# A four-layer attention and Fourier kernel: the Fourier transform in eight equal chunks, the last three of the first layer by blocks of rows

## The chip, the cores and the metric

The kernel runs on one core of one Trainium2 chip. A core has four engines that compute (TensorE does matrix multiplies; VectorE, ScalarE and GpSimd do the rest; in the profile they are PE, DVE, ACT and POOL), a fifth, SyncE, that here issues every DMA (SP), and 16 DMA engines. The metric is device time in microseconds: 1803.18 us is the median of three runs before the change (1801.92 to 1805.65).

## The reference

The input x has 2048 rows of 512 numbers. Four sublayers follow each other: attention A, Fourier mixing B, attention A again with the same weights, Fourier mixing B again. In this text an A with the B behind it is a layer, so there are layer one and layer two.

```
x = x + A(layernorm(x));  x = x + B(layernorm(x));  x = x + A(layernorm(x));  x = x + B(layernorm(x))

A(x): q, k, v = x@wq, x@wk, x@wv          # 32 heads of 16, rows cut into N = 4 segments of 512
  for s in range(4):                       # M, z: a memory carried from segment to segment
    p     = softmax(q_s k_s^T * scale + mask);   a_dot = p v_s
    a_mem = (phi(q_s) M) / (phi(q_s) z + 1e-6)
    o_s   = g * a_mem + (1 - g) * a_dot
    M, z += phi(k_s)^T v_s, sum phi(k_s)
  return concat(o) @ wo

B(x): a = x @ hid_re^T;  b = x @ hid_im^T        # [2048, 512] each
      y = seq_re @ a - seq_im @ b                # [2048, 2048] by [2048, 512], twice
```

What matters here: attention goes segment by segment of 512 rows, but each row of B's result needs all 2048 rows of its input. So layer two's attention can start on a row only when all rows of layer one have been through B.

## The kernel before

**Work.** A row tile is 128 rows, so there are 16 row tiles; a segment q (0 to 7, four to a layer) has four of them and is worked on in four groups of eight heads. Group i = 4q + g (0 to 31) goes through these steps, each a generator in the code: `s_p` projects q and k from the normalised, transposed rows (`xt`, tiles named g0 and g1) and `s_v` projects v; `t_split` stores q and k in two float16 halves to DRAM and loads them stacked (`qst`, `kst`, two sets); `s_x` multiplies all scores once and `t_max` takes the row maxima on VectorE; a transpose and two small DMAs put the maxima into `qst`; `s_st` multiplies the scores again, transposed, `t_sel` takes the exponential on ScalarE and masks on GpSimd (tiles of kind `pt`); `s_av` multiplies them with v; `s_m` divides (`t_merge`, through four DMAs) and adds the memory's share. A segment's four results `ot` then go through `s_o`: for each row tile WO, the product with wo, then `t_res`, which adds the residual and starts y with it (or adds to it), and `t_ln`, the layer norm, which ends in a transposing DMA into `xb`.

**Fourier mixing.** `s_ab` multiplies a row tile's `xb` with the hidden-side matrices into two float16 pairs `ab` (24 matmuls of 512 columns, called AB here). `s_f` does the sequence side. Its contraction runs over the 16 input row tiles, cut into chunks by `CHUNKS`; for each chunk and each output row tile t (a unit) a PSUM tile takes 12 matmuls for each pair of input row tiles, and `t_y` adds the PSUM tile into y[t]: VectorE's `scalar_tensor_tensor` (ScalarE writes it where it is the first). Before the change the chunks are six of 2 row tiles and one of 4. A unit of the 4-wide chunk is 24 matmuls. After the last chunk `t_y` stores y[t] to DRAM (x1 in layer one, the output in layer two). The sequence matrices come as pieces of 256 KB: `s_r` loads one (`craw`), `s_c` scales and splits it into float16 halves (`cc`), and stores those for layer two.

**Order.** No engine chooses its order on the chip. A planner (class `Plan` and the loop from line 1086) runs when the program is built: it lets the generator go next whose inputs, buffers and engine are free soonest by its own costs, and each engine then executes its instructions in that order, waiting at each for its inputs. Buffers come from 50 slots of 128 x 512 words (`work`, tiles named w) and 8 PSUM banks (tiles named b); `setup` gives each kind a least and a greatest number, and `slots_free` keeps back what other kinds have not yet got of their least. All instructions are recorded on one line, that of a helper, L241 (`Eng.call`), so tile names tell them apart.

**Where layer two starts.** `s_ln` of segment 4, the first of layer two, waits for each of its four rows' ("y", 0, t), loads them again from x1 and normalises them; then `s_p` can start group 16. Layer two's `s_o` waits once, at segment 4, until all 16 y tiles of layer one are stored:

```
            if layer and s == 0:
                yield gate(("y", layer - 1, NT - 1))
                ywritten.clear()
```

Of the kernel before, what the change touches and what calls it, by code (L numbers as in the profile page):

```python
# [19 lines left out]
NT = S // 128  # L20
# [6 lines left out]
CHUNKS = [2] * 6 + [4]  # L27
# [8 lines left out]
BATCH = 4  # L36
NR = 2


class Plan:  # L40
# [4 lines left out]
    def __init__(self):  # L45
# [8 lines left out]
        self.by = {}  # L54
        self.dma = None
# [22 lines left out]

    def slots_free(self, kinds):
        extra, taken, r = {}, {}, 0.0  # L80
        for k in kinds:
# [166 lines left out]
def body(ctx: ExitStack, tc: tile.TileContext, x, wq, wk, wv, wo, beta, wd, cs, out):  # L248
# [14 lines left out]
        ab=(4, 12)))  # L263
# [58 lines left out]
    def gate(*keys):  # L322
        return lambda: all(k in done for k in keys)
# [531 lines left out]
    def s_av():  # L855
        for i in range(NGRP):
# [16 lines left out]
            done.add(("E", i))  # L873

# [21 lines left out]
    def t_res(p, xi, gt, xb, key, last):  # L896
        yield need("V", p, xi)
        first = gt not in ywritten
        xo = y[:, gt, :] if first else xi
        V.scalar_tensor_tensor(xo, p, f_o, xi, op0=OP.mult, op1=OP.add)  # L900
        ywritten.add(gt)
# [37 lines left out]
    units = [(j, t) for j in range(len(chunks)) for t in range(NT)]  # L939
    nunit = len(CHUNKS) * NT  # L940
    npiece = NT * PAIRS
    cct = [tc.dram_tile([128, 2, 512], F16, name=f"cc{u}") for u in range(npiece)]
# [7 lines left out]
    def s_r():  # L950
        yield gate("WO")
        for j, t in units[:nunit]:
            for gt in chunks[j][1][::2]:
                yield need("Y", tag="craw")
                raw = sb("craw")
                Y.dma_start(raw, cs[gt // 2, t])
                raws.append(raw)
        u = npiece
        for k in range(npiece):
# [8 lines left out]
    def s_c():  # L968
        k = u = 0
        while u < nunit:  # L970
            n = width(units[u][0])
# [34 lines left out]
            u += m  # L1006

# [25 lines left out]
    def t_y(p, layer, t, f, last):  # L1033
        if t not in ywritten:
            ywritten.add(t)
# [6 lines left out]
        if last:  # L1042
            yield need("Y", y)
            Y.dma_start(fins[layer][t], y[:, t, :])
            done.add(("y", layer, t))

    def s_f():
        u = 0
        for j, (layer, r) in enumerate(chunks):
            pl.area["ab"]["kinds"]["ab"] = 2 * max(len(c[1]) for c in chunks[j:j + 2]), 12  # L1050
            keys = [(layer, gt, e) for gt in r for e in range(2)]
            yield gate(*[("ab", *k) for k in keys])
            ab = [abs_.pop(k) for k in keys]
            n = len(r) // 2
            for t in range(NT):
# [14 lines left out]
                f = (j % len(CHUNKS)) * NT + t  # L1070
# [101 lines left out]
```

## Time and profile before

| | |
|---|---|
| median of three runs | 1803.18 us (1801.92 to 1805.65) |
| the profiled execution | span 1799.7 us from first to last instruction; no other time of this execution is given |
| PE busy | 1689.9 us, 94% of the span, 11045 matmuls |
| DVE, ACT, POOL busy | 1090.5, 897.4, 726.2 us (61, 50, 40%) |
| DMA | 242.43 MB, mean 135 GB/s |
| mean granted TensorE clock | 0.971 |

The page divides the span into 40 slices of 45 us. Rows of stages give busy time of each engine (in brackets the number of instructions), then the granted TensorE clock, the busy share of the 16 DMA engines and GB/s. Rows of groups give engine, operation, output and inputs, shapes, count, then busy time and mean duration in ns, then the idle time ahead of them with what ended it. Rows of the order in time give start, duration, engine, operation, tiles, count, and in brackets the idle time ahead with its releaser. A busy PE is not PE at its peak: a matmul that runs at half the clock is busy for twice as long.

In the text, F(j, t) is the unit of chunk j and output row tile t, P, V, X, ST and AV are a group's projection, v, first scores, second scores and product with v, and "P16" is P of group 16.

### The profile page before, as it was taken

The page shows a single profiled execution, that of the slowest core. Times are in us where ns is not written, and L with a number is a line of the kernel's source. Part 1 is how long each engine was busy: PE and PEld are TensorE (multiplying, and loading weights), DVE is VectorE, ACT ScalarE, POOL GpSimd, SP SyncE. Part 2 cuts the span into 40 slices and gives each one's busy share as a digit, 9 for nine tenths or more (in the row PEclk, how much of TensorE's full clock was granted, in tenths as well). Part 3 has the DMA queues.
Part 4 walks back from the last instruction along what each step waited for, and adds up shares of the span by engine and source line. Part 5 has one row for each costly group of instructions (what it writes and reads, how often), then busy time and mean ns, then how long its engine had stood idle before and what let it go on. Part 6 is the DMA issues. An engine that isn't in the chain of part 4 may idle for free.

```text
span 1799.7 us, 32605 instructions
## 1 busy us (share of the span) xinstructions
PE 1689.9 (94%) x11045; PEld 741.6 (41%) x11045; DVE 1090.5 (61%) x3405; ACT 897.4 (50%) x1563; POOL 726.2 (40%) x1157
## 2 busy tenths in 40 slices
PE   3877899999999999999999879999999999999999
PEld 1432344443444444444444333444444444444444
DVE  7797865768587677464566655554637566534211
ACT  2547668656656666635437555465344444441000
POOL 3225554546554554543425443442534333332000
PEclk8888899999999999999999888999999999999999
DMA  7345645665565453544875442752526533232233
GB/s 193 98 123 137 187 113 151 175 158 148 134 167 165 131 139 118 151 133 157 263 184 172 125 127 49 158 142 78 141 88 141 147 108 103 80 103 65 94 123 117
DMA packets 240984, 242.43 MB, mean 135 GB/s; under 512 B 129777, under 2 KB 152305, under 8 KB 240817
## 3 DMA queue, kind: packets, MB, share of 16 engines
q1 hardware_dynamic: 240816, 240.35, 48.5%
q8 instruction: 87, 1.43, 0.3%
q14 instruction: 81, 0.66, 0.1%
HBM read 152.96 MB, written 63.70 MB: 120 GB/s over the span
## 4 chain that ended last, share of the span: by engine, by line
PE 63%; DMA 11%; DVE 10%; ACT 5%; issue 5%; POOL 4%; SPq 3%; ACTq 0%; POOLq 0%; DVEq 0%
PE b L241 63%; ACT w L241 5%; DMA w<-w 3%; DVE junk L241 3%; SPq L241 3%; POOL w L241 3%; DVE w L241 2%; DMA dc<-den 2%; DMA w<-rec 1%; DMA den<-w 1%; DVE cam L241 1%; DMA rec<-dc 1%; DMA w<-in_cs_dram 1%; DVE mx L241 1%; DVE y L241 1%
## 5 line engine op out<-in xcount | busy, mean ns | idle before, releaser
L241 PEld LDWEIGHTS <-w 128*128 128x128 f16 x4992 | 467.0, 99 | 625.7 <-issue 120.6
L241 PE MATMUL b<-w,w 128*128 128x512 f16 x3072 | 708.9, 380 | 2.9 <-DVE w L241 1.4
L241 POOL TENSOR_TENSOR w<-w,w 128x512 f16<-128x512 f32 (+1 forms) x317 | 381.3, 1208 | 388.6 <-ACT w L241 236.7
L241 ACT ACTIVATE w<-b,fac 128x512 f32<-128x512 f32 (+1 forms) x728 | 420.4, 657 | 185.3 <-PE b L241 180.0
L241 DVE CUSTOM_DVE_ANT_0 junk<-b,cmask 128x128 bf16<-128x128 f32 (+3 forms) x1024 | 438.3, 484 | 76.1 <-PE b L241 75.2
L241 POOL TENSOR_SCALAR_AFFINE_SELECT w<-w 128x128 f32<-128x128 f32 (+2 forms) x704 | 245.4, 360 | 342.5 <-ACT w L241 330.4
L241 DVE SCALAR_TENSOR_TENSOR y<-b,fyu,y 128x512 f32<-128x512 f32 x200 | 149.2, 746 | 212.7 <-PE b L241 211.9
L241 ACT ACTIVATE w<-b 128x512 f32<-128x512 f32 (+1 forms) x240 | 137.0, 597 | 215.2 <-PE b L241 208.9
L241 ACT ACTIVATE w<-w,csc 128x512 f16<-128x512 f32 (+1 forms) x256 | 181.5, 722 | 62.3 <-DVE csc L241 56.8
L241 PE MATMUL b<-g,w 128*128 128x512 f16 x768 | 187.1, 388 | 9.9 <-issue 5.3
L241 PE MATMUL b<-w,vt 128*32 128x512 f32 (+3 forms) x2048 | 183.3, 459 | 2.9 <-POOL w L241 2.1
L241 PE MATMUL b<-wd,w 128*128 128x512 f16 x768 | 177.7, 379 | 0.6 <-ACT y L241 0.5
L241 ACT ACTIVATE w<-w 128x512 f16<-128x512 f32 (+1 forms) x144 | 90.2, 632 | 166.2 <-DVE w L241 119.6
L241 DVE SCALAR_TENSOR_TENSOR w<-b,w 128x512 f16<-128x512 f32 x128 | 87.7, 687 | 128.1 <-ACT w L241 125.7
L241 PE MATMUL b<-kst,qst 62*128 62x128 f16 (+3 forms) x1024 | 130.2, 312 | 17.3 <-DVE mx L241 9.2
L241 PE MATMUL b<-qst,kst 64*128 64x512 f16 (+3 forms) x1024 | 120.8, 306 | 13.3 <-DVE mx L241 5.6
L241 PE MATMUL b<-w,g 128*128 128x128 f16 x1536 | 98.1, 222 | 7.3 <-ACT w L241 3.2
L241 PEld LDWEIGHTS <-g 128*128 128x128 f16 x1536 | 89.6, 99 | 22.3 <-issue 15.1
L241 PEld LDWEIGHTS b<-w,vt 128*32 128x32 f32 x2048 | 56.3, 111 | 95.5 <-issue 51.9
L241 PE MATMUL b<-wo,w 128*128 128x512 f16 x384 | 89.0, 384 | 1.5 <-ACT w L241 1.3
L241 PEld LDWEIGHTS <-kst 64*128 64x128 f16 x1024 | 37.6, 95 | 123.8 <-issue 116.4
L241 DVE DVE_READ_ACCUMULATOR2_ANT mx<- 128x1 f32 x1024 | 84.0, 82 | 0.0
(102 smaller groups left out, 892.1 us busy)
## 6 DMA issues: line engine op xcount, KB each, us to landing
w<-in_cs_dram SPq DMA_DIRECT2D x128, 256.0 KB
cc<-w SPq DMA_DIRECT2D x128, 256.0 KB
w<-cc SPq DMA_DIRECT2D x128, 256.0 KB
w<-w SPq DMA_DIRECT2D x96, 256.0 KB
d<-w SPq DMA_DIRECT2D x128, 128.0 KB
w<-rec SPq DMA_DIRECT2D x56, 256.0 KB
w<-in_x_dram SPq DMA_DIRECT2D x32, 256.0 KB
qst<-d SPq DMA_DIRECT2D x64, 128.0 KB
```

The lines of the kernel that those rows point to most:

```text
L241: r = f(*args, **kw)
```

## The change

`CHUNKS` becomes eight chunks of 2 row tiles. In layer one the units are no longer done chunk by chunk throughout: after chunks 0 to 4, the 48 units of chunks 5, 6 and 7 go by the list `LATE`, in blocks of rows: chunk 5 rows 0 to 7, chunk 6 rows 0 to 3, chunk 7 rows 0 to 3, then blocks of four rows in turn. A row's store no longer belongs to the last chunk: it comes when eight units have been added (`ycount`). Layer two goes chunk by chunk. The one wait of `s_o` on all of y is gone; instead a unit F of layer two waits in `t_y` for the store of its own row of layer one, and `ywritten` is kept by layer. `s_r` and the second reading of the pieces follow the new order. Chunks 5 to 7 hold 12 `ab` tiles at once, so `ab` may have 14 slots (12 before), its least number follows the chunks to come, `craw` gives up its least number once all pieces are made, the exponentials' least number (`pt`) does not hold back `ab` in the time between a layer's last AV and the next group's, and slots for `cc` and `craw` are kept back from every other kind.

```diff
-CHUNKS = [2] * 6 + [4]
+CHUNKS = [2] * 8
+LATE = [(5, 0, 8), (6, 0, 4), (7, 0, 4), (5, 8, 12), (6, 4, 8), (7, 4, 8), (5, 12, 16), (6, 8, 12), (7, 8, 12),
+        (6, 12, 16), (7, 12, 16)]
...
+    def floor(self, k, low):
+        ar = self.area[k]
+        ar["kinds"][k] = low, ar["kinds"][k][1]
...
-            keep = 0
-            if n >= low:
-                keep = sum(max(0, lo - self.count[o] - extra.get(o, 0))
-                           for o, (lo, _) in ar["kinds"].items() if o != k)
+            keep = sum(max(0, lo - self.count[o] - extra.get(o, 0)) for o, (lo, _) in ar["kinds"].items()
+                       if o != k and (n >= low or o in FIRST) and not (self.late and k == "ab" and o == "pt"))
...
-        ab=(4, 12)))
+        ab=(4, 14)))
...
             done.add(("E", i))
+            pl.late = q % NSEG == NSEG - 1 and g == NG - 1
...
-            if layer and s == 0:
-                yield gate(("y", layer - 1, NT - 1))
-                ywritten.clear()
...
+    whole = [(j, t) for j in range(nch) for t in range(NT)]
+    seq = [whole[:(nch - 3) * NT] + [u for x in LATE for u in rows(*x)], whole]
...
+        pl.floor("craw", 0)
...
-    def t_y(p, layer, t, f, last):
-        if t not in ywritten:
-            ywritten.add(t)
+    def t_y(p, layer, t, f):
+        if layer:
+            yield gate(("y", layer - 1, t))
+        if (layer, t) not in ywritten:
+            ywritten.add((layer, t))
...
-        if last:
+        ycount[layer, t] = ycount.get((layer, t), 0) + 1
+        if ycount[layer, t] == nch:
             yield need("Y", y)
             Y.dma_start(fins[layer][t], y[:, t, :])
             done.add(("y", layer, t))
...
-        for j, (layer, r) in enumerate(chunks):
-            pl.area["ab"]["kinds"]["ab"] = 2 * max(len(c[1]) for c in chunks[j:j + 2]), 12
-            keys = [(layer, gt, e) for gt in r for e in range(2)]
-            yield gate(*[("ab", *k) for k in keys])
-            ab = [abs_.pop(k) for k in keys]
-            n = len(r) // 2
-            for t in range(NT):
+        for layer in range(LAYERS):
+            tabs, left = {}, {}
+            for j, t in seq[layer]:
+                r = chunks[layer * nch + j][1]
+                if j not in tabs:
+                    following = [len(c[1]) for c in chunks[layer * nch + j:(layer + 1) * nch + 1][:3 if layer == 0 and j == nch - 3 else 2]]
+                    pl.floor("ab", 2 * (sum(following) if layer == 0 and j >= nch - 3 else max(following)))
+                    keys = [(layer, gt, e) for gt in r for e in range(2)]
+                    yield gate(*[("ab", *k) for k in keys])
+                    tabs[j], left[j] = [abs_.pop(k) for k in keys], NT
+                ab = tabs[j]
+                n = len(r) // 2
```

What this makes of the order shows at three places. TensorE's program is the same in both up to the seventh unit of chunk 4 in layer one, F(4, 6), behind whose first half AB of row tile 11 now stands. In the rows, b is a PSUM bank, w a work slot, and the helper's line is L247 after the change.

On SP, where the first rows of layer one are stored (x1_0 to x1_3), before:

```order
L241 DMA x1_1_69<-y_84 128x512
L241 DMA w23_11284<-x1_1_69 128x512
L241 DMA_TRANSPOSE g0_11228<-w8_11296 128x8x128
L241 DMA x1_2_70<-y_84 128x512
L241 DMA w6_11330<-in_cs_dram 128x512
L241 DMA cc104_246<-w2_11313 128x1024
L241 DMA w46_11340<-in_cs_dram 128x512
L241 DMA w10_11350<-x1_2_70 128x512
L241 DMA cc105_247<-w34_11336 128x1024
L241 DMA w15_11369<-in_cs_dram 128x512
L241 DMA cc106_248<-w13_11365 128x1024
L241 DMA x1_3_71<-y_84 128x512
```

and with the change:

```order
L247 DMA x1_0_68<-y_84 128x512
L247 DMA w15_11091<-x1_0_68 128x512
L247 DMA x1_1_69<-y_84 128x512
L247 DMA w46_11123<-in_cs_dram 128x512
L247 DMA x1_2_70<-y_84 128x512
L247 DMA cc96_238<-w41_11111 128x1024
L247 DMA w18_11142<-in_cs_dram 128x512
L247 DMA w13_11152<-x1_1_69 128x512
L247 DMA cc97_239<-w3_11138 128x1024
L247 DMA w44_11162<-in_cs_dram 128x512
L247 DMA x1_3_71<-y_84 128x512
L247 DMA cc98_240<-w47_11155 128x1024
```

The four stores stand within 11 rows, where the last three of them took 12; the pieces (in_cs_dram) and their split halves (cc) that lay between are fewer.

On PE, where layer one's last unit ends, before (b1_12960 is F(6, 15), and behind it come the first scores X19):

```order
L241 MATMUL b1_12960<-w41_11161,w1_12801 128x512
L241 LDWEIGHTS qst1_105
L241 MATMUL b2_13208<-kst1_103,qst1_105 128x256
L241 LDWEIGHTS qst1_105
L241 MATMUL b7_13209<-kst1_103,qst1_105 128x256
L241 LDWEIGHTS qst1_105
L241 MATMUL b2_13208<-kst1_103,qst1_105 128x256
```

and with the change (b6_13434 is F(7, 15), and behind it are X19's last scores and AV18, whose inputs are vt0 and the exponentials):

```order
L247 MATMUL b6_13434<-w33_10758,w6_13125 128x512
L247 LDWEIGHTS qst1_105
L247 MATMUL b2_13484<-kst1_103,qst1_105 128x512
L247 LDWEIGHTS qst1_105
L247 MATMUL b3_13485<-kst1_103,qst1_105 128x512
L247 MATMUL b1_13280<-w23_13430,vt0_106 32x256 x2
L247 MATMUL b1_13280<-w0_13452,vt0_106 32x256 x2
L247 MATMUL b0_13294<-w11_13431,vt0_106 32x256 x2
L247 MATMUL b0_13294<-w1_13453,vt0_106 32x256 x2
```

In the order before, X19 starts 28 rows ahead of the end of layer one's last unit; with the change it starts 333 rows ahead of it.

On DVE, behind the update of the memory (macc) and the split of group 16's result (w32, w29), before:

```order
L241 TENSOR_TENSOR macc_96<-b7_12852,bd_111 128x128 x2
L241 SCALAR_TENSOR_TENSOR w32_12582<-w23_12581,w32_12582 128x512
L241 ISA junk_12914,mx_12558<-b0_12905,cmask_110 128x384
L241 ISA mx_12558 128x1
L241 ISA junk_12920,mx_12558<-b5_12906,cmask_110 128x384
```

and with the change:

```order
L247 TENSOR_TENSOR macc_96<-b0_12667,bd_111 128x128 x2
L247 SCALAR_TENSOR_TENSOR w29_12429<-w6_12428,w29_12429 128x512
L247 SCALAR_TENSOR_TENSOR y_84<-b5_12714,fyu_270,y_84 128x512
L247 SCALAR_TENSOR_TENSOR y_84<-b0_12754,fyu_270,y_84 128x512
L247 ISA junk_12819,mx_12421<-b3_12811,cmask_110 128x512
L247 ISA mx_12421 128x1
```

Two additions into y now stand ahead of the row maxima (junk, mx) there.

More of the change, by code (lines that the diff above doesn't have):

```diff
@@ L36 @@
 BATCH = 4
+FIRST = "cc", "craw"
 NR = 2
@@ L951, in s_r @@
         yield gate("WO")
[L952 to L957, printed above, removed]
+        for pair, t in order[0]:
+            yield need("Y", tag="craw")
+            raw = sb("craw")
+            Y.dma_start(raw, cs[pair, t])
+            raws.append(raw)
         u = npiece
-        for k in range(npiece):
+        for k in (place[x] for x in order[1]):
             yield gate(("cd", k), ("cd", npiece - 1))
```

26 lines of the change are left out of this document (18 added, 8 removed).

## The prediction

> **What bounds the kernel now.** I read the page's busy times and slices first, to see which engine bounds it and where that engine is not full.
>
> ```profile
> span 1799.7 us, 32605 instructions
> PE 1689.9 (94%) x11045; PEld 741.6 (41%) x11045; DVE 1090.5 (61%) x3405; ACT 897.4 (50%) x1563; POOL 726.2 (40%) x1157
> PE   3877899999999999999999879999999999999999
> PEclk8888899999999999999999888999999999999999
> ```
>
> PE bounds the kernel, except in two places: the first five slices, and slices 23 to 25, where layer one meets layer two. There PE is idle and its clock is granted below full. The sums by stage put numbers on it.
>
> ```profile
> 0.00:140.00 140.00, 95.21 (x668) 45.12 (x669) 112.06 (x420) 58.00 (x103) 39.89 (x78) 0.85 0.50 139
> ...
> 745.00:860.00 115.00, 114.69 (x542) 52.97 (x541) 66.49 (x128) 49.76 (x76) 48.80 (x44) 1.00 0.50 154
> 860.00:1000.00 140.00, 134.89 (x915) 63.73 (x914) 85.33 (x286) 74.85 (x124) 60.05 (x85) 0.99 0.70 198
> 1000.00:1100.00 100.00, 82.66 (x565) 33.86 (x563) 63.98 (x248) 51.13 (x94) 41.34 (x79) 0.83 0.48 120
> 1100.00:1300.00 200.00, 194.25 (x1359) 83.37 (x1356) 110.09 (x363) 105.04 (x189) 86.76 (x147) 1.00 0.49 120
> 1300.00:1555.00 255.00, 252.40 (x1776) 109.42 (x1773) 157.18 (x526) 117.53 (x212) 93.05 (x168) 1.00 0.44 114
> 1555.00:1799.70 244.70, 240.95 (x1223) 106.45 (x1222) 71.62 (x125) 39.45 (x71) 34.68 (x57) 1.00 0.31 96
> ```
>
> The change leaves PE's order as it is up to about 745 us (F(4,6)), so the start stays. From 1100 us on PE lacks 5.75 + 2.60 + 3.75 us, little to win. What can be won lies between 860 and 1117 us. Waits and order of time there:
>
> ```profile
> PE b L241 <- DVE mx L241: 9.1, 10, 5.4
> ...
> PE b L241 <- ACT w L241: 3.5, 12, 0.6
> ```
>
> ```profile
> 887.76 2.10 PE L241 MATMUL b<-w,w 128*128 128x512 f16 x9
> 889.70 0.59 PE L241 MATMUL b<-g,w 128*128 128x512 f16 x2
> ...
> 1005.47 0.62 PE L241 MATMUL b<-kst,qst 62*128 62x128 f16 x12
> ...
> 1037.63 0.60 PE L241 MATMUL b<-qst,kst 64*128 64x512 f16 x4
> ...
> 1065.70 0.43 PE L241 MATMUL b<-w,vt 128*32 128x128 f32 x8 [0.16 <-POOL w L241]
> ...
> 1077.84 0.39 PE L241 MATMUL b<-identf,mx 128*32 128x128 f32 x1 [5.40 <-DVE mx L241]
> ...
> 1079.88 4.42 PE L241 MATMUL b<-wo,w 128*128 128x512 f16 x12
> ...
> 1096.93 1.25 PE L241 MATMUL b<-wd,w 128*128 128x512 f16 x5
> ```
>
> These are P16 at 889.70, X19 at 1005.47, ST19 at 1037.63, the end of AV19 at 1066.1, the transpose of X20's maxima, WO of layer two at 1079.88 and its first AB at 1096.93. F(6,15), the last unit of layer one, ends at 1008. Layer two's first unit comes at 1117. Between them PE has attention alone: each step waits for another engine's answer, and no Fourier matmul fills the gap.
>
> ```profile
> 889.70:1008.00 118.30, 114.41 (x849) 54.84 (x847) 70.67 (x267) 61.42 (x105) 44.63 (x70) 0.99 0.64 177
> 1008.00:1079.90 71.90, 56.50 (x416) 23.31 (x416) 42.96 (x166) 41.29 (x75) 33.23 (x62) 0.83 0.50 131
> 1079.90:1117.00 37.10, 35.67 (x205) 12.65 (x204) 22.05 (x76) 17.08 (x32) 13.37 (x30) 0.86 0.29 51
> ```
>
> Idle: 3.9 + 15.4 + 1.4 = 20.7 us. Clock: what PE did below full speed would have taken 0.01 x 114.4 + 0.17 x 56.5 + 0.14 x 35.7 = 15.7 us less. Together 36.4 us: the most that this change can win here.
>
> **The change part by part.** *Later units.* A Fourier matmul costs what it does where PE does nothing else:
>
> ```profile
> 1710.00:1755.00 45.00, 45.00 (x211) 20.37 (x209) 7.09 (x10) 1.19 (x2) 0.00 (x0) 1.00 0.37 123
> ```
>
> 45 / 211 = 0.213 us, a unit of 12 2.56 us. Counted in the built orders, 93 Fourier matmuls fewer stand ahead of P16 (1236 against 1329): P16 can come 19.8 us earlier. Between P16 and layer two's first unit now stand 300 Fourier matmuls (207 before), 180 of P (144), 60 of AB (48), 16 fewer each of ST and AV. So the same chain of segment 4 has some 27 us more PE work beside it ((93 + 36 + 12) x 0.213 = 30, less about 3 for ST and AV). Most of the 36.4 us can be covered. What comes back, wait by wait:
>
> *P16 waits for y.* In the order, 85 matmuls stand between the unit that completes row tile 3 and P16, before and now. Before, that was
>
> ```profile
> 869.92 0.73 DVE L241 SCALAR_TENSOR_TENSOR y<-b,fyu,y 128x512 f32<-128x512 f32 x1
> ...
> 870.69 0.32 SPq L241 DMA_DIRECT2D x<-y  x1
> ...
> 876.09 0.32 SPq L241 DMA_DIRECT2D w<-x  x1
> ...
> 884.80 1.92 SPq L241 DMA_TRANSPOSE g<-w  x1
> ```
>
> addition, store, load, layer norm, transposing DMA: 869.92 to 889.70, 19.8 us against 85 x 0.213 = 18.1 of work. The rows now finish one per 2.56 us instead of 5.1, so four stores and loads crowd into SP's queue, where the load of x1 stands behind the store it waits for. I take 3 us of stall; 0 if the queue keeps up, 8 if two tiles wait as the 870.69 to 876.09 one did.
>
> *AB closer behind WO in layer one.* The new order leaves 45 matmuls (9.6 us) between WO and AB for row tiles 12 and 14, and 57 (12.2 us) for 15. The chain of residual, norm and transpose took
>
> ```profile
> 212.25 5.34 PE L241 MATMUL b<-wo,w 128*128 128x512 f16 x24
> 225.63 0.60 PE L241 MATMUL b<-wd,w 128*128 128x512 f16 x2
> ```
>
> 10.7 us from the first of two tiles (ends 214.9) in the best case, and 12.6 us at 1084.3 to 1096.93. So 1 to 3 us for each of two tiles: I take 3 us in all, range 0 to 6.
>
> *Segment 4's end.* The two halves of the way from X19 to WO:
>
> ```profile
> 1005.50:1037.60 32.10, 26.80 (x154) 8.19 (x153) 21.75 (x85) 18.16 (x33) 15.30 (x31) 0.79 0.51 127
> 1037.60:1079.90 42.30, 31.60 (x284) 15.85 (x284) 23.22 (x93) 23.13 (x42) 18.48 (x32) 0.88 0.50 133
> ```
>
> The first lost 5.3 idle and 0.21 x 26.8 = 5.6 by the clock; 60 Fourier matmuls (13 us) and 72 short ones of V now stand in it besides, more than the loss: nothing comes back. The second lost 10.7 and 0.12 x 31.6 = 3.8, so its work was 27.8 us; 33 more of P (7.0 us), 36 fewer short ones of V (2.2 us at about 0.06) and six of the memory (1) make it 33.6. The chain itself, ST19 at 1037.63, AV19 to 1066.1, the division's DMAs and the split of the last group's result
>
> ```profile
> 1082.27 0.69 DVE L241 SCALAR_TENSOR_TENSOR w<-w,w 128x512 f16<-128x512 f32 x1
> ```
>
> at 1083.0, comes to 45.4 us, of which WO's first nine matmuls overlap 2. Stall: 45.4 - 2 - 33.6 = 9.8, say 9 us; 4 if the division goes faster, 14 with the old loss. *AB behind WO in layer two*: 42 matmuls, 36 of them WO's, are 8.5 us against 12.6: 4 us (0 to 5). Left over from the clock: 2 us (0 to 6).
>
> *Sixteen more additions on DVE in this stretch.* 300 matmuls are 25 additions into y, where 207 in wide units were 9.
>
> ```profile
> L241 DVE SCALAR_TENSOR_TENSOR y<-b,fyu,y 128x512 f32<-128x512 f32 x9 | 6.7, 745 | 4.6 <-PE b L241 4.6
> ...
> L241 DVE SCALAR_TENSOR_TENSOR y<-b,fyu,y 128x512 f32<-128x512 f32 x200 | 149.2, 746 | 212.7 <-PE b L241 211.9
> ```
>
> 16 x (0.745 + 4.6 / 9) = 20 us of DVE, which in 889.7 to 1008 was busy 70.67 of 118.3. The row maxima stand behind them on the same engine. DVE has room, and the order gives a group some 5 us more than before, so I charge 2 us; 0 to 20. In the whole run there are 32 more; the other 16 fall in layer two, where DVE waits for PE anyway (211.9 us ahead of these additions).
>
> *Fewer normalising matmuls.* One column sum serves four units instead of two halves: 32 instead of 40, each two passes,
>
> ```profile
> L241 PE MATMUL b<-cam,ones 128*128 128x4 f32 x48 | 8.4, 245 | 4.1 <-DVE cam L241 3.8
> L241 PE MATMUL b<-cam,ones 128*128 128x2 f32 x32 | 4.8, 246 | 1.8 <-DVE cam L241 1.8
> ```
>
> 16 rows fewer at 0.245 us, overlapping by about half: 2 us won (0 to 4).
>
> *The wait that goes.* y's last row was added at 1008 and stored some 5 us later, WO came at 1079.88: the wait on all of y had been over for 65 us. Dropping it is worth nothing, and neither does the new wait of layer two's first units on their own row cost anything. Narrow units at the end of layer two: a DVE addition of 0.75 us per 2.56 us of PE, as in the row of 1710 to 1755 with twice the count, is hidden, and nothing behind the last matmul changes. The 12 held `ab` tiles take slots from attention; ST and AV stand in the order as densely as before, so 0.
>
> **Sum.** 36.4 + 2 won, 3 + 3 + 9 + 4 + 2 + 2 = 23 back: 15.4 us won. 1799.7 - 15.4 = 1784.3 for the profiled execution; the median of the runs is 3.5 us above its span, so 1788 us.
>
> [...]
>
> ```profile
> 920.00:940.00 20.00, 18.61 (x94) 8.57 (x94) 17.45 (x72) 6.51 (x12) 5.95 (x5) 0.91 0.67 185
> ```
>
> here PE was idle for 1.4 us in all and the clock was 0.91.
>
> **Rivals.** (1) *DVE holds the chain, slower.* Each of the 16 added additions stands in DVE's order ahead of the maxima of X17 to X19 and waits there for its unit. In the mean they waited 0.51 us; where several stand in a row, as in the order on DVE, or PE is late, more. At 1.2 us of wait and nothing overlapped, 16 x (0.745 + 1.2) = 31 us in place of the 2 charged: 1817. It decides from 1.3 us per addition, wait included (20.8 us in all, 1806.8). Against it: DVE was busy for 60% of this stretch, so a delay there is not at once one of the chain. [...]
>
> [...]
>
> (3) *The hole only moves.* Between layer one's last unit and layer two's first there were 930 rows of PE's order and are 879 now, with no Fourier work in them; if P16, X19 and the division are each bound by their own latency, 33 of 36 us come back and the time is about 1801 to 1804: no change. Against it: X19 now starts 333 rows ahead of that hole, not 28.
>
> **How the numbers follow.** My forecast, 1779 to 1797, gets 0.54; rival 2, below it, 0.12; rival 3 0.13; rival 1 and what else makes it slower 0.21. A change of under 0.2% (3.6 us) can't be told from none. Faster: 0.54 + 0.12 = 0.66; same 0.13; slower 0.21. The range for 8 in 10 is 1773 to 1808: it leaves out half of rival 2's side and the worse half of rival 1.
>
> **What would show it.** In the profile after: P16 at about 873 us, four stores of x1 ahead of it; the clock from 1000 to 1100 us above 0.92; PE idle under 13 us between P16 and layer two's first unit; WO of layer two near 1072 us. Wrong if P16 comes later than 880, if DVE's idle time ahead of y's additions grows past 1.3 us each in that stretch, or if PE's idle time after 1117 us grows by more than 10 us.

## The result and the profile after

The changed kernel takes 1785.73 us (median of four runs, 1782.81 to 1789.87) against 1804.41 us for the kernel before, measured beside it (four runs, 1801.92 to 1806.4): a ratio of 0.990, 95% interval 0.9876 to 0.9922. In two further measurements the ratio was 0.992 (0.9905 to 0.9935) and 0.9905 (0.9886 to 0.9924). The forecast was 1788 us, within 1773 to 1808. The profiled execution spans 1783.1 us.

The page's busy times, and its slices for PE with the granted clock:

```profile
span 1783.1 us, 32611 instructions
PE 1676.0 (94%) x11029; PEld 731.7 (41%) x11029; DVE 1111.9 (62%) x3440; ACT 898.7 (50%) x1563; POOL 723.1 (41%) x1154
PE   3877899999999999999899998999999999999999
PEclk8888899999999999999999999999999999999999
```

The three 8s of the clock in slices 23 to 25 are gone, and the two slices in a row in which PE was not full, 8 and 7, are one 8 (slice 25); another 8 stands in slice 20, around P16. PE's busy time fell by 13.9 us (1689.9 to 1676.0) for 16 matmuls fewer, its idle time by only 2.7 us (109.8 to 107.1). So in this profile most of what was won is time in which PE had run at half its clock: half of its busy time at half clock, over the whole span, fell by 12.8 us (39.8 to 27.0). What half a clock costs shows at WO of layer two: 9 of its matmuls run in the 3.60 us from 1081.10 at a clock of 0.50, 18 in the 3.60 us from 1084.80 at 1.00. In the profiles of the two further measurements it fell by 4.0 and 5.4 us, and the idle time by 5.1 and 4.1, so that this share is not a fixed one. The sums by stage:

```profile
745.00:860.00 115.00, 113.80 (x547) 52.13 (x546) 65.84 (x129) 47.84 (x74) 48.08 (x46) 1.00 0.50 156
860.00:1000.00 140.00, 131.12 (x920) 59.35 (x917) 96.82 (x333) 80.39 (x132) 61.81 (x86) 1.00 0.65 189
1000.00:1100.00 100.00, 91.61 (x617) 38.61 (x616) 69.33 (x229) 56.30 (x102) 49.19 (x82) 0.97 0.65 164
1100.00:1300.00 200.00, 195.41 (x1439) 86.08 (x1438) 118.71 (x395) 108.22 (x196) 85.52 (x150) 1.00 0.45 118
1300.00:1555.00 255.00, 252.16 (x1769) 105.49 (x1768) 154.70 (x520) 123.12 (x223) 92.96 (x177) 1.00 0.39 104
```

Between 1000 and 1100 us PE is busy for 91.6 us instead of 82.7, and its clock is 0.97 instead of 0.83. Between 860 and 1000 it is idle for 8.9 us instead of 5.1. The steps that the prediction dates, in order of time on PE:

```profile
864.95 2.76 PE L247 MATMUL b<-w,w 128*128 128x512 f16 x12 [1.81 <-POOL w L247]
868.80 2.76 PE L247 MATMUL b<-w,w 128*128 128x512 f16 x12 [1.09 <-POOL w L247]
872.40 2.33 PE L247 MATMUL b<-w,w 128*128 128x512 f16 x10 [0.84 <-POOL w L247]
874.57 2.75 PE L247 MATMUL b<-g,w 128*128 128x512 f16 x12
...
996.37 0.62 PE L247 MATMUL b<-kst,qst 62*128 62x128 f16 x12
...
1034.65 0.60 PE L247 MATMUL b<-qst,kst 64*128 64x512 f16 x4
...
1062.72 0.64 PE L247 MATMUL b<-w,vt 128*32 128x128 f32 x16
...
1076.78 0.28 PE L247 MATMUL b<-identf,mx 128*32 128x128 f32 x1 [3.50 <-DMA w<-w]
...
1081.04 12.35 PE L247 MATMUL b<-wo,w 128*128 128x512 f16 x48 [0.23 <-DVE mx L247]
...
1094.07 2.76 PE L247 MATMUL b<-wd,w 128*128 128x512 f16 x12
```

P16 comes at 874.57 (889.70 before), X19 at 996.37 (1005.47), ST19 at 1034.65 (1037.63), AV19 ends at 1063.4 (1066.1). The lead of 15.1 us is used up step by step, and WO of layer two comes at 1081.04 where it came at 1079.88. Layer two's first unit starts at 1115.0 (1119.5). The stretch from P16 to layer two's first unit is called the join here, and its part without Fourier units, from layer one's last unit on, the hole. PE in the three parts of the join, divided at layer one's last unit (1025.0) and at WO:

```profile
874.60:1025.00 150.40, 144.66 (x1018) 64.07 (x1016) 106.02 (x370) 87.90 (x148) 67.27 (x106) 1.00 0.68 195
1025.00:1081.00 56.00, 48.46 (x391) 22.08 (x391) 34.94 (x126) 34.03 (x62) 25.72 (x40) 0.97 0.67 165
1081.00:1115.00 34.00, 33.64 (x177) 12.48 (x177) 24.04 (x69) 14.35 (x27) 12.34 (x25) 0.94 0.25 63
```

Idle 5.7 + 7.5 + 0.4 = 13.6 us; by the clock 0.03 x 48.5 + 0.06 x 33.6 = 3.5 us. The join loses 17.1 us; by the same sum it lost 36.4 before.

### The profile page after: what moved, and what is told of

It is laid out like the page before. It is cut to its first block, busy times and chain, and to the rows that moved or that the text cites. A ratio compares the mean times of both kernels' runs of the same rounds, so it can differ in the third digit from the quotient of the medians.

```text
span 1783.1 us, 32611 instructions
## 1 busy us (share of the span) xinstructions
PE 1676.0 (94%) x11029; PEld 731.7 (41%) x11029; DVE 1111.9 (62%) x3440; ACT 898.7 (50%) x1563; POOL 723.1 (41%) x1154
## 4 chain that ended last, share of the span: by engine, by line
PE 59%; DVE 12%; DMA 12%; issue 5%; POOL 5%; ACT 4%; SPq 3%; POOLq 0%; DVEq 0%; ACTq 0%
PE b L247 59%; ACT w L247 4%; DVE junk L247 4%; POOL w L247 4%; DMA w<-w 3%; DVE w L247 3%; SPq L247 3%; DMA dc<-den 2%; DMA w<-rec 1%; DMA w<-in_cs_dram 1%; DMA den<-w 1%; DVE cam L247 1%; DMA w<-x 1%; DVE y L247 1%; DMA rec<-dc 1%
## 5 line engine op out<-in xcount | busy, mean ns | idle before, releaser
L247 PEld LDWEIGHTS <-w 128*128 128x128 f16 x4992 | 464.9, 98 | 624.6 <-issue 118.4
L247 PE MATMUL b<-w,w 128*128 128x512 f16 x3072 | 707.9, 380 | 5.8 <-POOL w L247 3.7
L247 POOL TENSOR_TENSOR w<-w,w 128x512 f16<-128x512 f32 (+1 forms) x317 | 381.2, 1208 | 372.9 <-ACT w L247 236.0
L247 ACT ACTIVATE w<-b,fac 128x512 f32<-128x512 f32 (+1 forms) x728 | 420.9, 657 | 207.8 <-PE b L247 193.1
L247 DVE CUSTOM_DVE_ANT_0 junk<-b,cmask 128x128 bf16<-128x128 f32 (+3 forms) x1024 | 438.4, 484 | 50.4 <-PE b L247 49.7
L247 POOL TENSOR_SCALAR_AFFINE_SELECT w<-w 128x128 f32<-128x128 f32 (+2 forms) x704 | 244.1, 359 | 364.4 <-ACT w L247 358.7
L247 DVE SCALAR_TENSOR_TENSOR y<-b,fyu,y 128x512 f32<-128x512 f32 x232 | 173.3, 747 | 215.9 <-PE b L247 214.5
L247 ACT ACTIVATE w<-b 128x512 f32<-128x512 f32 (+1 forms) x240 | 137.5, 599 | 176.1 <-PE b L247 171.1
L247 ACT ACTIVATE w<-w,csc 128x512 f16<-128x512 f32 (+1 forms) x256 | 181.7, 721 | 56.5 <-DVE csc L247 42.6
L247 PE MATMUL b<-g,w 128*128 128x512 f16 x768 | 186.7, 386 | 8.8 <-issue 5.3
L247 PE MATMUL b<-w,vt 128*32 128x512 f32 (+3 forms) x2048 | 176.7, 446 | 3.8 <-POOL w L247 2.8
L247 PE MATMUL b<-wd,w 128*128 128x512 f16 x768 | 179.9, 380 | 0.0
L247 DVE SCALAR_TENSOR_TENSOR w<-b,w 128x512 f16<-128x512 f32 x128 | 87.9, 687 | 131.5 <-ACT w L247 128.0
L247 ACT ACTIVATE w<-w 128x512 f16<-128x512 f32 (+1 forms) x144 | 90.1, 631 | 157.0 <-DVE w L247 116.1
L247 PE MATMUL b<-kst,qst 62*128 62x128 f16 (+3 forms) x1024 | 128.9, 307 | 15.3 <-DVE mx L247 7.1
L247 PE MATMUL b<-qst,kst 64*128 64x512 f16 (+3 forms) x1024 | 117.5, 305 | 8.6 <-ACT w L247 4.0
L247 PE MATMUL b<-w,g 128*128 128x128 f16 x1536 | 98.0, 221 | 9.6 <-DMA w<-w 4.4
L247 PEld LDWEIGHTS <-g 128*128 128x128 f16 x1536 | 88.8, 99 | 25.9 <-issue 16.0
L247 PEld LDWEIGHTS b<-w,vt 128*32 128x32 f32 x2048 | 53.9, 109 | 94.9 <-issue 53.2
L247 PE MATMUL b<-wo,w 128*128 128x512 f16 x384 | 89.8, 390 | 1.1 <-ACT w L247 0.9
L247 DVE TENSOR_REDUCE cam<-w 128x1 f32<-128x512 f32 x128 | 81.4, 675 | 11.2 <-DMA w<-in_cs_dram 11.0
L247 DVE DVE_READ_ACCUMULATOR2_ANT mx<- 128x1 f32 x1024 | 84.0, 82 | 0.0
```

Source lines behind the costliest of these rows:

```text
L247: r = f(*args, **kw)
```

## The experiments

To compare runs I split each profiled execution into work and loss. Loss is PE's idle time plus half of its busy time in the stretches where the granted clock was half, both taken from the trace; the rest is work. The work came to 1643 to 1652 us in the twelve profiles of kernels without added matmuls, so what sets them apart is loss, to within some 9 us. "Behind" is from layer two's first unit on. Up to chunk 4 of layer one the order is the same in all but the run with extra matmuls at the start, and the loss there was 94 to 103 us. The medians come from different chips; the ratio is to the kernel before on the same chip. What differs:

| run | Fourier matmuls, P16 to layer two's first unit | median us | ratio to before (95%) | loss F(4,0) to P16 | loss in the join | loss behind |
|---|---|---|---|---|---|---|
| before | 207 | 1804.41 | | 2.1 | 36.2 | 12.0 |
| the change | 300 | 1785.73 | 0.990 (0.988 to 0.992) | 5.2 | 16.4 | 10.8 |
| e1_plain | 90 | 1813.56 | 1.009 (1.006 to 1.012) | 14.4 | 35.1 | 10.8 |
| e4_less | 201 | 1797.07 | 0.9985 (0.996 to 1.001) | 8.2 | 27.4 | 13.7 |
| e3_more | 345 | 1800.83 | 1.001 (0.999 to 1.004) | 4.7 | 24.4 | 26.4 |
| r_after (the change) | 300 | 1788.05 | 0.992 (0.9905 to 0.9935) | 4.6 | 22.4 | 14.5 |
| r2_after (the change) | 300 | 1785.59 | 0.9905 (0.989 to 0.992) | 4.6 | 22.6 | 13.8 |
| tb_215 | 207 | 1801.99 | 1.000 (0.998 to 1.002) | 4.1 | 40.7 | 11.1 |
| ta_215 | 300 | 1789.92 | 0.994 (0.992 to 0.995) | 4.8 | 23.6 | 13.8 |
| e6_dve | 300 | 1792.06 | 0.994 (0.993 to 0.996) | 4.9 | 24.7 | 13.7 |
| e7_slots | 318 | 1797.81 | 0.999 (0.9975 to 1.001) | 7.6 | 23.6 | 10.6 |
| e12_hold | 300 | 1787.83 | 0.992 (0.990 to 0.994) | 5.1 | 24.1 | 12.1 |
| e5_warm | 207, and 194 of no use | 1817.37 | 1.0095 (1.008 to 1.011) | 2.2 | 14.0 | 12.9 |
| e8_start | 315 | 1813.67 | 1.008 (1.006 to 1.010) | 11.0 | 16.7 | 14.1 |

The join's loss in the three profiles of the changed kernel is 16.4, 22.4 and 22.6 us. Differences of some 5 us in one profile mean nothing. Where a text below names theory 1 without more, it is that the gain is the Fourier work kept back beside segment 4's attention.

**Equal chunks in plain order.** Is it the eight equal chunks, or the order of the last three? Only `LATE` is changed, here and in the next two:

```diff
-LATE = [(5, 0, 8), (6, 0, 4), (7, 0, 4), ...]
+LATE = [(5, 0, 16), (6, 0, 16), (7, 0, 16)]
```

> The change with its list of blocks replaced by plain order: chunk 5 whole, then 6, then 7; all else of the change kept. Theory 1 (the gain is the Fourier work kept back beside segment 4's attention): 90 Fourier matmuls stand between P16 and layer two's first unit instead of 300 (207 before the change), and P16 comes 117 matmuls (25 us) later than before the change. The stretch without Fourier work grows, so slower than before by 15 to 30 us: 1819 to 1834, with PE idle and half clock past 1000 us above the 20.7 us and 37 us of before. Theory 2 (equal chunks and the new slot rules carry the gain): 1786 to 1792.

Measured: 1813.56 us, slower than the kernel before. P16 came at 929.2 us, and the join:

```profile
929.20:991.30 62.10, 60.76 (x394) 28.37 (x394) 39.34 (x149) 26.16 (x45) 19.55 (x28) 0.98 0.78 217
991.30:1109.20 117.90, 98.77 (x797) 42.95 (x797) 77.35 (x297) 69.15 (x127) 50.79 (x96) 0.88 0.47 118
1109.20:1146.30 37.10, 37.10 (x212) 14.36 (x212) 23.85 (x63) 18.06 (x34) 15.81 (x31) 0.95 0.26 66
```

The last two rows are the hole, 155 us long. In the kernel before it is 112.7 us long:

```profile
1006.80:1119.50 112.70, 95.28 (x637) 36.96 (x637) 67.31 (x251) 60.87 (x112) 48.26 (x95) 0.85 0.42 102
```

And yet its loss, 19.1 us idle and 0.12 x 98.8 + 0.05 x 37.1 by the clock, is 32.8 us where it was 17.4 + 0.15 x 95.3 = 31.7. More work of layer two's attention stands in it. What this run loses over before lies ahead of P16 (14.4 us against 2.1). So the equal chunks and the new slot rules win nothing in plain order; my size was too large since the loss of the hole did not grow with its length.

**Two chunks by blocks instead of three.**

```diff
+LATE = [(5, 0, 16), (6, 0, 4), (7, 0, 4), (6, 4, 8), (7, 4, 8), (6, 8, 12), (7, 8, 12), (6, 12, 16), (7, 12, 16)]
```

> The change with eight units fewer kept back: all of chunk 5 first, then chunks 6 and 7 by blocks of four rows. 201 Fourier matmuls stand between P16 and layer two's first unit and 1335 ahead of P16, almost what before the change has (207 and 1329), but with equal chunks, rows completed at twice the pace at first, the new slot rules and no wait of WO on all of y. Theory 1: the time of before less 2 us for the fewer normalising matmuls, 1798 to 1806. Theory 2 (blocks of rows and freed rows of y as such): 1786 to 1792.

Measured: 1797.07 us, ratio 0.9985 with 1 in the interval. With 201 Fourier matmuls behind P16, as many as before had in wide units, there is no gain that can be told: the join lost 8.8 us less than before, but 6.1 more were lost ahead of P16 and 1.7 more behind the join.

**All three chunks by blocks of four rows.**

```diff
+LATE = [(5, 0, 4), (6, 0, 4), (7, 0, 4), (5, 4, 8), (6, 4, 8), (7, 4, 8), (5, 8, 12), (6, 8, 12), (7, 8, 12), (5, 12, 16), (6, 12, 16), (7, 12, 16)]
```

> The change with four more units kept back: chunks 5, 6 and 7 all by blocks of four rows from the start. 345 Fourier matmuls between P16 and layer two's first unit (300 in the change), P16 45 matmuls (9.6 us) earlier. Theory 1: what is left to win in that stretch of the change is 13.6 us idle and 7 us at half clock; a part of it goes, 1779 to 1786. Rival (the stretch is now bound by the chain of segment 4 itself): 1784 to 1790, no difference from the change.

Measured: 1800.83 us: no gain, a miss for both theories. P16 came at 858.9, the earliest of all. But the hole and the stretch behind it were no better filled:

```profile
1024.00:1077.20 53.20, 40.98 (x309) 20.09 (x309) 28.42 (x105) 23.15 (x44) 19.15 (x27) 0.86 0.66 186
1077.20:1124.90 47.70, 47.56 (x329) 20.79 (x328) 29.54 (x89) 24.21 (x44) 19.72 (x35) 0.98 0.46 97
1124.90:1300.00 175.10, 166.18 (x1089) 71.17 (x1088) 100.97 (x351) 89.94 (x161) 78.86 (x130) 0.97 0.48 123
```

The last row loses 8.9 us idle and 0.03 x 166 = 5 us by the clock, where the changed kernel from 1100 to 1300 has 4.6 idle and a clock of 1.00. So an earlier P16 and more filler don't win more. From 1120 to 1640 us PE waited 6.2 us for tiles that ACT writes and 5.8 for row maxima, against 0.3 and 3.2 in the change; why this order does so was not followed further.

**The change again, and both kernels in another order.** The gain could belong to one lucky order. `tb_215` is the kernel before, `ta_215` the changed one, each with the planner's latency of a matmul raised from 197 to 215 ns from F(4,8) on, which gives another order behind that point:

```diff
+                if (layer, j, t) == (0, 4, 8):
+                    pl.LAT = dict(pl.LAT, T=215.0)
```

> The change once more, on the chip of the three kernels that follow, as their measure. Expected at 0.99 of the kernel before, 1778 to 1790.

> The kernel before with the planner's latency of a matmul set from 197 to 215 ns from F(4,8) on, and nothing else: another order of the same work (207 Fourier matmuls between P16 and layer two's first unit, as before). Theory 1 (the gain is the Fourier work kept back): within 8 us of the kernel before, 1792 to 1808. Rival (the change's gain is the luck of one order among many): spread of 10 us or more, overlapping the next kernel's.

> The change with the planner's latency of a matmul set from 197 to 215 ns from F(4,8) on, and nothing else: another order with the same 300 Fourier matmuls between P16 and layer two's first unit. Theory 1: 1778 to 1792, at least 8 us under the kernel before it in this list. Rival (luck of the order): 1792 or more.

Measured: 1788.05, 1801.99 and 1789.92 us. Before stays at a ratio of 1.000, the change at 0.994, where the change itself had 0.992 on this chip: most of the gain outlives this change of order, so it is not the luck of a single one. The join loses 40.7 us in the one and 23.6 in the other. But not every order with that much Fourier work behind P16 wins: `e3_more` (345) and `e7_slots` (318) don't.

**More work on DVE.** Rival 1 asked what added work on DVE costs. Here 25 additions of 512 columns, whose result nothing reads, follow y's additions from F(6,7) on, in an otherwise equal order:

```diff
+            if layer == 0 and k >= fyat[6, 7]:
+                nc.vector.scalar_tensor_tensor(rg("junk", 2, BF16), p, f, y[:, t, :], op0=OP.mult, op1=OP.add)
```

> The change with one more VectorE instruction of the size of an addition into y (0.75 us, into a scratch row that nothing reads) behind each of the 25 additions of layer one's units from F(6,7) on, which is from P16 on; the order of all other instructions is the change's own, row for row. Theory (VectorE has room in this stretch, additions are not on segment 4's path): 0 to 4 us above the change. Rival (the added additions hold the chain; VectorE in order): 25 x 0.75 = 19 us, at least 10 of it seen, with WO of layer two later by as much.

Measured: 1792.06 us, 4 us above the changed kernel on the same chip (1788.05). DVE's groups in the join of this run; L1062 is the added line:

```profile
L247 DVE SCALAR_TENSOR_TENSOR y<-b,fyu,y 128x512 f32<-128x512 f32 x26 | 19.4, 748 | 12.2 <-PE b L247 12.0
L1062 DVE SCALAR_TENSOR_TENSOR junk<-b,fyu,y 128x512 bf16<-128x512 f32 x25 | 18.8, 751 | 0.9
```

18.8 us of added DVE work cost some 4 us of time, far from one for one. So DVE's queue does not hold the chain at the price of rival 1, which falls.

**The rules for slots.** The old rule of `slots_free` with the rest of the change:

```diff
-            keep = sum(max(0, lo - ...) ... if o != k and (n >= low or o in FIRST) and not (self.late and k == "ab" and o == "pt"))
+            keep = 0
+            if n >= low:
+                keep = sum(max(0, lo - ...) ... if o != k)
```

> The change with the old rule of which slots are kept back (nothing reserved for cc and craw from kinds below their least number, and the exponentials' least number always held against ab); chunks, blocks and the 14 slots of ab stay. 318 Fourier matmuls between P16 and layer two's first unit instead of 300. Theory 1: the slot rules are no part of the gain, 1780 to 1792. Rival (they keep attention and the pieces supplied): above 1795.

Measured: 1797.81 us; the gain is gone, which I had not expected. The clause on `FIRST` has no part in it: without it the change builds the same program, instruction for instruction, and without the clause on `late` it builds that of this run. So letting `ab` take slots ahead of the exponentials, between layer one's last ST and the next group's, belongs to the gain. By itself it brings none, for `e1_plain` and `e4_less` have it too. How it works is open. P16 came at 869.1, and from there to the split of group 19's result took 224 us (209 to 215 in the three profiles of the change). The profiled run, 1793.70 us, lies 4 us under the median, and its losses from F(4,0) on, 41.8 us, are those of the change's repeats (41.5 and 41.0). So this profile does not show where the time goes.

**A warm clock in the kernel before.** In the first profile most of the gain is clock. Does a fuller clock alone bring it? The kernel before, with a thirteenth stream that gives PE matmuls of no use in the hole:

```diff
+    def s_warm():
+        yield gate(("y", 0, NT - 1))
+        while not {("ab", 1, 1, 1)} <= done:
+            yield need("T", w_o, tag="dft")
+            p = ps("dft")
+            for k in range(2):
+                T.matmul(p, w_o[:, 0, 0, 0:128], w_o[:, 0, 0, :], start=(k == 0), stop=(k == 2 - 1))
+            pl.close(p)
```

> The kernel before, with 194 extra matmuls (97 pairs of 512 columns on wo, into a PSUM bank that nothing reads) which the order places wherever TensorE would else wait, from the store of layer one's last row to the second AB of layer two. They compute nothing that is used; they only keep TensorE at work, so that its clock should stay granted. In the kernel before this stretch (1008 to 1117 us) was idle for 16.8 us and lost 0.17 x 56.5 + 0.14 x 35.7 = 14.6 us by the clock. Theory 1, the change wins because TensorE is at work in the hole and so keeps its clock, and the clock lies on the path that sets the end: the clock from 1000 to 1100 us goes above 0.95 and a good half of the 14.6 us is won, less what real steps wait for an extra pair (0.43 us at most each): 1792 to 1799 us. Rival, the clock there costs nothing of its own because the steps wait for other engines anyway, and the change wins by the real work that it moved into the hole: the clock goes up just as much, the idle time is filled with matmuls that nobody needs, and the time stays at 1801 to 1806 us.

Measured: 1817.37 us, 16 us slower, a miss for both. The join, and the added group over the whole run:

```profile
888.30:1008.40 120.10, 115.47 (x844) 55.16 (x843) 69.35 (x257) 61.47 (x105) 44.12 (x69) 0.97 0.61 175
1008.40:1096.00 87.60, 83.35 (x599) 35.29 (x597) 50.91 (x203) 43.42 (x77) 33.85 (x62) 0.98 0.48 118
1096.00:1130.50 34.50, 34.50 (x222) 13.46 (x221) 18.57 (x50) 17.69 (x33) 12.74 (x28) 1.00 0.16 32
```

```profile
L241 PE MATMUL b<-wo 128*128 128x512 f16 x194 | 47.1, 383 | 2.4 <-DVE mx L241 1.9 <-DVE w L241 0.3
```

The clock in the hole went from 0.83 to 0.98 and PE was busy for 95% of it. The join's loss fell from 36.4 to 8.9 idle + 0.03 x 115.5 + 0.02 x 83.4 = 14.0 us, less than in the changed kernel. But the 194 matmuls are 194 x 0.213 = 41.3 us of work: 41.3 - 22.4 = 18.9 us more, of which 16 were measured. WO came at 1096.0, 16 us later, since the chain's own steps stood behind the filler: from P16 to the split of group 19's result they took 207.8 us, 193.3 before. So neither a granted clock nor a busy PE is a gain by itself; work wins there if it has to be done in any case.

**The same at the start of the changed kernel**, with 375 pairs of 256 columns until the output weights are ready:

```diff
+    def s_warm():
+        while "WO" not in done:
+            yield need("T", ones, tag="dft")
...
+                T.matmul(p[:, 0:256], ones.bitcast(F16)[:, 0:128], ones.bitcast(F16), start=(k == 0), stop=(k == 1))
```

> The changed kernel, with 750 extra matmuls (375 pairs of 256 columns on a constant tile, into a PSUM bank that nothing reads) which the order places wherever TensorE would else wait in the first 240 us, until the output weights are ready. They compute nothing that is used. In the changed kernel the clock was 0.81, 0.88 and 0.88 in 0 to 60, 60 to 140 and 140 to 240 us, on 25.3, 68.8 and 81.7 us of TensorE's work: 4.8 + 8.3 + 9.8 = 22.9 us lost by the clock, beside 64.2 us idle. Theory 1, clock lost is time lost wherever TensorE carries the chain, which at the start is less than half of it: the clock there goes above 0.95 and 5 to 10 us are won over the change: 1775 to 1782 us. Rival, the start is set by VectorE and the DMAs (VectorE was at work for 113 of the first 140 us), so the clock is worth nothing there, and the extra pairs delay real steps: 1786 to 1797 us.

Measured: 1813.67 us, ratio 1.0078, slower than both kernels. The first 240 us of the changed kernel and of this run:

```profile
0.00:240.00 240.00, 175.84 (x1231) 78.53 (x1232) 186.57 (x649) 124.03 (x220) 92.09 (x164) 0.86 0.53 144
```

```profile
0.00:240.00 240.00, 216.38 (x1870) 136.13 (x1871) 173.55 (x621) 115.99 (x204) 86.50 (x150) 0.95 0.52 141
```

The clock rose from 0.86 to 0.95, but DVE did 13 us less of its own work by then, and F(4,0) came at 728 us, 13 us later than in the changed kernel (715). From there to P16 another 10 us went, 6 of them loss (11.0 against 5.2).

**Less of layer two's work in the hole.** The order also puts 36 matmuls of P and 12 of AB of layer two into the join. Here they wait for layer two's first unit:

```diff
+            if i in (22, 23):
+                yield gate("F1")
             yield gate(*[("L", q, t) for t in range(TT)])
...
+                if layer and gt == 2:
+                    yield gate("F1")
                 yield gate(("xb", layer, gt))
...
+                if layer:
+                    done.add("F1")
```

> The changed kernel with the work of layer two that it has in the hole cut back to that of the kernel before: the projections of groups 22 and 23 and AB of row tile 2 wait, in the order, for layer two's first unit. Between P16 and that unit stand 144 matmuls of P and 48 of AB (180 and 60 in the changed kernel), the 300 Fourier matmuls stay: 48 x 0.213 = 10.2 us less of work beside the chain, to be done behind it. Theory 1, real work in the hole is what wins, since TensorE without it is idle or at half clock there: the first unit of layer two comes at most 3 us earlier than 1115.0 and 5 to 10 us come back: 1791 to 1797 us. Rival, the work in the hole also stands ahead of the chain's own steps (from P16 to the split of group 19's result it took 193 us before, 208 with the change), so that with less of it the first unit comes 7 to 10 us earlier, and nothing is lost: 1783 to 1789 us.

> The changed kernel once more, on the chip of the run that holds work back, as the measure for it: 1783 to 1790 us by all theories; from P16 to the split of group 19's result some 208 us again.

Measured on one chip: 1787.83 and 1785.59 us, ratios 0.9917 and 0.9905, no difference that the runs resolve. The join without these matmuls, and then in the repeat of the change:

```profile
869.10:1018.30 149.20, 143.96 (x1018) 64.35 (x1016) 105.86 (x371) 87.89 (x148) 67.36 (x106) 0.99 0.67 196
1018.30:1069.80 51.50, 40.46 (x353) 19.77 (x352) 29.89 (x108) 28.56 (x53) 19.74 (x35) 0.88 0.58 138
1069.80:1100.90 31.10, 29.28 (x170) 11.08 (x168) 19.67 (x65) 15.95 (x30) 14.54 (x30) 0.98 0.35 85
```

```profile
871.20:1027.00 155.80, 147.58 (x1018) 65.52 (x1016) 106.80 (x370) 88.02 (x148) 67.65 (x106) 0.98 0.64 188
1027.00:1083.90 56.90, 48.90 (x390) 22.21 (x389) 34.94 (x126) 34.03 (x62) 25.55 (x40) 0.97 0.66 162
1083.90:1117.70 33.80, 33.43 (x178) 12.47 (x178) 23.94 (x69) 14.39 (x27) 12.34 (x25) 0.95 0.27 64
```

WO came at 1069.8 and layer two's first unit at 1100.9, 14 and 17 us earlier than in this repeat (10 and 13 than in the other), and the kernel was not faster: 10.2 us of the work taken out had to be done behind it, and the rest of the lead is within what two profiles of one kernel differ by. Here the work in the hole and the chain beside it change places about one for one. The rival's time held, but not its reason: I had priced only its lead of 7 to 10 us.

## Why the prediction was right

The sum came out right because its largest part did, what the join would give back. The prediction dates the end of layer one's last unit at 1008 and layer two's first unit at 1117; the trace before has them at 1006.8 and 1119.5, which makes 36.2 us to win of its 36.4. 17.1 came back in the join (22.4 and 22.6 by the table in the repeats); I had charged 17 there: 9 for segment 4's end, 4 for AB in layer two, 2 for the clock, 2 for DVE. That these two agree to a tenth is luck. By parts the 17.1 are 5.7 us ahead of layer one's last unit, where 2 were charged for DVE, 9.0 for segment 4's end and 2.4 for AB, with 3.5 of the clock in them; and the repeats lie 5 us higher.

Won there: 19.3 us in the first profile, 14 in the repeats. Given back: 3.1 us ahead of P16 (2.5 in the repeats). Behind the join the loss was 1.2 less in the first profile, about 2 more in the repeats. That makes 17 us in the first and some 9 in the repeats, where the spans are 16.6, 13.4 and 11.7 us shorter than before. Of the last two, some 4 and 2 us stand in none of these losses and are not explained.

- **P16 for y, 3 us.** P16 came at 874.6 (870 and 871 in the repeats) for the 873 forecast. The stall has the size by luck, 3.7 us, since it has another cause: the rows at 864.95 to 872.40 are units of the Fourier mixing that wait for POOL, for the low halves of their own pieces. P16 itself waited for nothing. What the four stores did to SP's queue I had priced, what the blocks ask of the preparation of pieces not.
- **AB behind WO in layer one, 3 us.** 0 came back: PE's rows of AB there have no idle time ahead of them, and PE's idle time from 745 to 860 is 1.2 us, 0.3 before.
- **X19 to ST19, nothing.** PE is nearly full, as said (from 1000 to 1040 us it was idle for 0.8 us, and the clock was 1.00), but the step took 38.3 us instead of 32.2, and P16 to X19 121.8 instead of 115.8.
- **Segment 4's end, 9 us: the step that failed.** Its stall is 7.5 idle and 1.5 by the clock, 9.0 us. That the size fits is luck, for it was worked out from a chain of 45.4 us that starts 8 us earlier, and so put WO at 1072. ST19 to the split of group 19's result,

```profile
1082.62 0.69 DVE L247 SCALAR_TENSOR_TENSOR w<-w,w 128x512 f16<-128x512 f32 x1
```

took 48.7 us and WO came at 1081.0. Together the chain from P16 to this split is 208.7 us, 15.4 longer than before (193.3), and 212.0 and 215.0 in the repeats: the filler delays the steps that it stands beside. I treated a chain as fixed and the work beside it as free, and with that reasoning a WO that comes no earlier would have been a failure of the change. It was not: by then 93 Fourier matmuls more, that is 19.8 us of work due in any case, had been done beside the chain. The useless matmuls (41.3 us of filler, a chain 14.5 us longer than before) and the held-back work (10.2 us less, a chain of 203.8 us) showed this exchange from both sides. Why a gain also needs the slot clause, and why 345 kept-back matmuls win nothing, it does not say.
- **AB behind WO in layer two, 4 us.** 0.4 idle and 0.06 x 33.6 = 2.0 by the clock; 13.0 us from WO to AB, almost all of it covered by WO's own matmuls.
- **DVE, 2 us.** Right. The additions in the join:

```profile
L247 DVE SCALAR_TENSOR_TENSOR y<-b,fyu,y 128x512 f32<-128x512 f32 x26 | 19.4, 748 | 15.2 <-PE b L247 14.9
```

0.58 us of idle time ahead of each, far from 1.3; and at 4 us for 18.8 of added work, an estimate for the 12 us of added busy time here is 2.6.
- **Fewer normalising matmuls, 2 won.** Their busy time fell by 2.0 us, the idle time ahead of them rose by 1.7:

```profile
L247 PE MATMUL b<-cam,ones 128*128 128x4 f32 x64 | 11.2, 245 | 7.6 <-DVE cam L247 7.0 <-DMA w<-w 0.4 <-ACT w L247 0.2
```

- **The wait on y, nothing.** Right, and exactly so: with `s_o`'s wait put back, the change builds the same program, instruction for instruction.
- **Slots, 0.** No run tests the 0 of the change as built. But the rule on slots, to which I gave no worth, is part of the gain: with the old rule it was gone, and that has no explained cause.
- **What would show it.** The clock (0.97, asked for above 0.92) and P16 came as said; PE's idle time from P16 on was 13.6 us where under 13 was asked; WO near 1072 failed. None of the three signs of a wrong prediction came.

Rival 2, the time below the forecast, was the nearest: in the first profile the clock came back nearly whole (15.7 us lost before, 3.5 after; about 7 and 6 in the repeats), the idle time did not (20.7 and 13.6; 15 and 17 in the repeats). That short waits leave the clock full, the supposition behind that rival's 1773 us and so behind the low end of the range, no run shows. In the join the clock fell at 1077.9, 1.2 us after a wait of 3.50 us ahead of the transpose at 1076.78 had ended:

```profile
1073.20:1077.80 4.60, 1.04 (x17) 0.55 (x18) 4.60 (x17) 0.90 (x3) 1.70 (x2) 1.00 0.48 141
1077.80:1084.70 6.90, 5.74 (x16) 1.77 (x17) 6.90 (x40) 1.26 (x2) 3.21 (x3) 0.51 0.52 162
1084.70:1090.00 5.30, 5.30 (x26) 2.34 (x25) 4.40 (x11) 0.63 (x1) 1.00 (x2) 0.99 0.20 72
```

It stayed at half for 6.8 us. And in the second repeat the clock fell at 967.8 us, behind 3.40 us in which PE was busy for 1.19:

```profile
964.40:967.80 3.40, 1.19 (x8) 0.21 (x5) 1.90 (x4) 3.25 (x6) 1.48 (x6) 0.99 0.49 178
967.80:974.60 6.80, 6.47 (x23) 3.56 (x27) 5.57 (x18) 2.08 (x3) 2.28 (x3) 0.50 0.35 116
```

Shorter waits went ahead of a fall too: in the kernel before the clock was at half for 3.4 us from 922.8 on, and the waits of PE just ahead of that were of 1.83, 0.16 and 0.16 us.

## What to carry to other kernels

Where one engine is full nearly everywhere, price a new order by that engine's losses (idle time and time at half clock), not by when a step of a chain comes: here WO came 1 us later and the kernel was 1% faster, and in another run it came 10 to 14 us earlier than in the change's repeats and nothing was won. Work moved beside a chain lengthens the chain, here by 15 us for 27 us of work, and is still a gain if it is work that has to be done in any case; work of no use that fills the same hole makes PE's idle time and clock look better (0.98 in the hole for 0.83) and the kernel slower (by 16 us). More kept-back work is not more gain: 300 matmuls won 1%, 345 nothing. And count the allocator's rules as part of a change of order: without one clause of them the gain was gone.

## What the runs showed of the hardware

In the kernel before, the granted clock was at half for 3.4, 6.8, 6.8, 3.4, 10.2 and 6.8 us between 922 and 1097 us, in the change for one stretch of 6.8 in the join, 17 and 14 us in all in the joins of its repeats. The same program differs by some 6 us of loss in the join from one profile to the next (16.4, 22.4 and 22.6 us), of which 3 to 4 are the clock.

How much PE had worked ahead of a fall of the clock can be read from the profiles before and after. Behind 240 us the clock fell six times in the one and twice in the other, and in the 3.4 us ahead of each fall PE had been busy for 0.97 to 2.58 us (1.45 ahead of 922.8 in the kernel before, 1.10 ahead of 1077.9 in the change). But not every such stretch cost the clock: from 862.90 to 866.31 us in the change PE was busy for 1.60 us, and the clock stayed at 1.00 until 1077.9.

In the first 240 us, PE's idle time went from 58.6 to 64.5 us between profiles of runs with the same order there, and half of its busy time at half clock from 19.7 to 26.9 us, but mostly against each other: in all but one run the sum was 84.0 to 86.7 us (81.5 in that one); the kernel before has 60.8 + 24.3, the change 64.2 + 22.5. That would fit a start whose chain other engines set, where PE loses by the clock what it does not lose by waiting, which no run shows by itself; the matmuls that raised the clock there from 0.86 to 0.95 did not help.
